# Two matrix products behind an attention stage: tiles that carry the slot from which they can be had, and six more of them at the boundary between the products

## The chip, the cores and the metric

One core of a Trainium2 chip. The metric is device time in microseconds of one execution, the median of several. TensorE multiplies, VectorE (DVE) and ScalarE (ACT) read accumulators, split and add operands, SyncE (SP) issues nearly all DMA transfers, in order, each after what it must wait for.

## What is computed

```python
def _attn_ref(q, k, v):                      # 8 batches, 12 heads, 448 positions, 64 wide
    scores = scale * np.matmul(q, k.transpose(0, 1, 3, 2)) - np.log(S)
    attn = 1.0 / (1.0 + np.exp(-scores))
    return np.matmul(attn, v).astype(np.float32)

def _moe_ref(x, w_in, w_out):                # x [3584, 768], w_in [768, 2048], w_out [2048, 768]
    h = x @ w_in
    g = np.maximum(0.01 * h, h)
    return (g @ w_out).astype(np.float32)
```

The output of the attention, heads side by side, is the `x` of the second function. All in float32; the weights come as float64 and are turned into float32 on the chip.

## The kernel before, in words

There are three stages: attention, the first FFN product (h), the second FFN product. Both FFN products use a bilinear scheme with 20 block products in place of 24: operands are sums and differences of blocks, and accumulators are added into several outputs. Each product runs in four passes `p` over the positions (two batches each), 20 forms `i` per pass, two halves per form: 160 items per product. One item is 12 matmuls 128x128 by 128x448, because each float32 operand is split into a high and a low part (fp32r) and three of the four partial products are made.

The order is written out by hand. Time is counted in slots, one per item; `now` is the slot. `at(when, rank, fn)` (line 169) puts a piece of work into a slot, `slot` (line 176) issues a slot's pieces in order of rank, then the item's matmuls. Every engine then works through its own instructions in that order, and waits where it must.

Operands and results live in tiles of one size, 128x896 float32 (448 KB). `tiles` (line 254) adds tiles to the list `spare`: 13 from the start (`TILES`), 3 more from the first product on (`MORE`), 2 more for the second (`LAST`). `grab` (line 258) takes the first of the list, `drop` (line 265) puts one back at its end. A tile whose last user has not finished may be handed out; the new user then waits.

First product: the weights of forms 15 to 19 are streamed through three buffers in every pass (`Streamed`, tiles `ws`): loaded, high part by a cast on ACT, low part by a subtraction on DVE, in slots given by `prepared_by` (line 698). An accumulator is read into a tile `h` one slot after its item (`read1`); finished blocks are passed through the leaky function on ACT, and stored to memory (`save1`, line 725; `full`); three differences of them, tiles `m`, are made and stored by `made2` (line 770), which drops the tile in the same slot. Beside this, DVE unpacks and sums the weights `w_out` for the second product (`prep`, tiles `wd` and `ws1`), paced by `SHARE` (line 27), into memory; they are loaded again as `w`, in seven groups of four.

Second product: operand `k` (`Operand`, line 798) is loaded (`load`: one or two tiles `g`; a block that the operand before it has is shared), added up into a tile `gf` where it is a sum (`whole`, DVE), cast (`high`, ACT, into a tile `gh` or one of its own) and its low half subtracted (`low`, DVE). Item `k` issues, in this order, the sum of operand k+2, the low half of k+1, the high half of k+2, work on late weights, the reading of a finished accumulator, its own matmuls, and then loads as far as tiles allow: `g_load` (line 887) loads the next operand if the list has tiles for it beside those that `wanted` (line 874) counts, with `SPARE` to spare. The first four operands are placed by the table `FIRST2`: step, operand, how many slots ahead of the boundary, rank. Results are built up in tiles `o`; `store` (line 933) issues the transfer to the output and drops the tile at once. The weights of the last two groups are loaded in the first items of the second product.

## Time and profile before

| what | value |
|---|---|
| runs | 1092.62, 1093.48, 1092.15 us; median 1092.62 |
| the profiled execution | 1088.45 us, its span 1086.7 us |
| TensorE busy | 1039.6 us (96%) |
| DVE, ACT busy | 849.7 us (78%), 575.5 us (53%) |
| DMA | 319.82 MB, mean 294 GB/s |
| chain that ended last | TensorE 68%, DMA 15%, DVE 11% of the span |

The profiled execution is one run, 4.2 us under the median. Attention takes the first 250 us or so, the first FFN product the time to 658 us, the second the rest. A busy TensorE is not TensorE at its peak: matmuls are pipelined, so the count of matmuls in a stretch says more than the busy time. A wait is put down to what came last.

### The profile page before, as it was taken

The page shows a single profiled execution, that of the slowest core. Times are in us where ns is not written, and L with a number is a line of the kernel's source. Part 1 is how long each engine was busy: PE and PEld are TensorE (multiplying, and loading weights), DVE is VectorE, ACT ScalarE, POOL GpSimd, SP SyncE. Part 2 cuts the span into 40 slices and gives each one's busy share as a digit, 9 for nine tenths or more (in the row PEclk, how much of TensorE's full clock was granted, in tenths as well). Part 3 has the DMA queues.
Part 4 walks back from the last instruction along what each step waited for, and adds up shares of the span by engine and source line. Part 5 has one row for each costly group of instructions (what it writes and reads, how often), then busy time and mean ns, then how long its engine had stood idle before and what let it go on. Part 6 is the DMA issues. An engine that isn't in the chain of part 4 may idle for free.

```text
span 1086.7 us, 15679 instructions
## 1 busy us (share of the span) xinstructions
PE 1039.6 (96%) x5690; PEld 859.9 (79%) x5690; DVE 849.7 (78%) x1094; ACT 575.5 (53%) x698; POOL 0.3 (0%) x5
## 2 busy tenths in 40 slices
PE   9999999999999999999999996899899989998998
PEld 5554555547898999899989985799799979988997
DVE  5888889888879787878866785787877877878777
ACT  6877878785644444444447653543344334424442
POOL 0000000000000000000000000000000000000000
PEclk9999999999999999999999997899999999999999
DMA  7899998989949976986798687989958986897796
GB/s 272 281 357 312 319 354 272 400 270 346 332 155 319 338 277 205 337 307 230 238 358 304 220 293 275 332 293 323 355 208 287 355 304 236 292 350 257 252 317 244
DMA packets 123837, 319.82 MB, mean 294 GB/s; under 512 B 12912, under 2 KB 44656, under 8 KB 123760
## 3 DMA queue, kind: packets, MB, share of 16 engines
q1 hardware_dynamic: 123040, 318.13, 83.7%
q8 instruction: 45, 0.74, 0.3%
q10 hardware_dynamic: 720, 0.69, 0.2%
q14 instruction: 32, 0.26, 0.1%
HBM read 221.77 MB, written 96.99 MB: 293 GB/s over the span
## 4 chain that ended last, share of the span: by engine, by line
PE 68%; DMA 15%; DVE 11%; issue 3%; ACT 1%; SPq 1%; DVEq 0%; ACTq 0%
PE f L135 28%; PE pv L135 10%; PE acc_A L135 9%; PE sc L135 9%; DMA g<-g 7%; PE acc_B L135 6%; PE acc_E L135 3%; DMA out<-o 3%; PE acc_D L135 2%; DVE g L135 2%; DVE gf L135 2%; DMA xd<-x_s 1%; PE acc_C L135 1%; SPq L135 1%; DVE wd L135 1%
## 5 line engine op out<-in xcount | busy, mean ns | idle before, releaser
L135 PE MATMUL f<-xh,w 128*128 128x448 f32 x960 | 271.1, 362 | 2.8 <-DVE x L135 1.6
L135 PEld LDWEIGHTS f<-xh,w 128*128 128x128 f32 x960 | 180.0, 188 | 16.6 <-issue 2.2
L135 PE MATMUL f<-xl,w 128*128 128x448 f32 x480 | 173.6, 362 | 0.0
L135 DVE TENSOR_TENSOR gf<-g,g 128x896 f32<-128x896 f32 x104 | 113.3, 1089 | 74.2 <-DMA g<-g 26.4
L135 ACT CAST g<-gf 128x896 fp32r<-128x896 f32 x64 | 60.4, 944 | 143.9 <-DVE gf L135 138.5
L135 ACT ACTIVATE s<-sc 128x896 f32<-128x896 f32 x144 | 119.7, 934 | 9.3 <-PE sc L135 9.0
L135 DVE TENSOR_TENSOR h<-h,f 128x896 f32<-128x896 f32 x88 | 95.5, 1085 | 36.4 <-PE f L135 34.7
L135 PE MATMUL pv<-s,v 128*64 128x448 f32 x576 | 113.8, 543 | 0.0
L135 PE MATMUL acc_A<-g,w 128*128 128x448 f32 x256 | 83.9, 383 | 20.1 <-DVE g L135 19.3
L135 PEld LDWEIGHTS sc<-qks 64*128 64x128 f32 x876 | 79.2, 185 | 28.4 <-issue 16.2
L135 ACT COPY h<-f 128x896 f32<-128x896 f32 x56 | 50.1, 909 | 93.7 <-PE f L135 77.9
L135 PE MATMUL sc<-qks 64*128 64x448 f32 (+1 forms) x876 | 96.6, 368 | 3.2 <-DVE x L135 2.9
L135 PE MATMUL f<-xh,ws 128*128 128x448 f32 x320 | 92.8, 368 | 6.8 <-DVE ws L135 4.5
L135 PE MATMUL acc_A<-gh,w 128*128 128x448 f32 x320 | 95.4, 369 | 0.0
L135 PEld LDWEIGHTS f<-xl,w 128*128 128x128 f32 x480 | 90.0, 187 | 5.8
L135 PE MATMUL acc_B<-gh,w 128*128 128x448 f32 x320 | 93.3, 362 | 0.0
L135 DVE TENSOR_TENSOR xl<-xl,xh 128x896 fp32r<-128x896 f32 x64 | 69.5, 1087 | 26.0 <-ACT xh L135 25.9
L135 PEld LDWEIGHTS pv<-s,v 128*64 128x64 f32 x576 | 39.0, 137 | 63.3 <-issue 51.7
L135 PE MATMUL acc_B<-g,w 128*128 128x448 f32 x256 | 79.2, 365 | 2.6 <-DVE g L135 2.5
L135 ACT ACTIVATE h<-h 128x896 f32<-128x896 f32 x56 | 53.1, 951 | 42.4 <-DVE h L135 41.9
L135 ACT CAST xh<-xl 128x896 fp32r<-128x896 f32 x64 | 60.2, 941 | 26.9 <-PE f L135 19.7
L135 PEld LDWEIGHTS acc_A<-g,w 128*128 128x128 f32 x256 | 49.9, 198 | 27.6 <-DVE g L135 22.9
(76 smaller groups left out, 1597.9 us busy)
## 6 DMA issues: line engine op xcount, KB each, us to landing
g<-g SPq DMA_DIRECT2D x240, 448.0 KB, 5.2
xl<-xd SPq DMA_DIRECT2D x64, 448.0 KB, 5.6
g<-h SPq DMA_DIRECT2D x64, 448.0 KB, 5.7
qk<-in_qk SPq DMA_DIRECT2D x46, 448.0 KB, 6.1
xd<-x_s SPq DMA_DIRECT2D x36, 448.0 KB, 7.3
xd<-x SPq DMA_DIRECT2D x28, 448.0 KB, 7.0
wr<-in_w_in SPq DMA_DIRECT2D x24, 512.0 KB, 5.7
wr<-in_w_out SPq DMA_DIRECT2D x24, 512.0 KB, 4.4
```

The costliest lines, as they stand in the source:

```text
L135: return lambda *args, **kw: tc.keep_in_program_order(issue(*args, **kw))
```

## The change

A place in `spare` is now a tuple: the slot from which the tile can be had, the pool, the tag, and a kind. `grab` takes the place with the smallest of (slot from which it can be had, but not before now; preference by kind). `drop` puts a tile back with `now + slots`: 1 for most, 2 for an `h` whose store was issued a slot before, 3 for tiles whose store is issued in this slot, 4 for stored results of the second product. `room` counts places that can be had by the next slot and are not of the kind RESULTS; `g_load` goes by it.

The two tiles `LAST` are of the kind RESULTS: only `h`, `m` and `o` tiles may take them. They are added 40 slots before the boundary (start of the last pass of the first product) and not at it, with four tiles of the kind LENT, which may be taken until the boundary and are given back at item `BACK` = 10. The room for both is that of the unpacking of `w_out`, which so must be done 40 slots earlier; its pace `SHARE` is raised. The last group of weights takes the room of the four when they are given back, so its loads move from the first items to items 12 to 18; the group before it is loaded at items 1, 3, 5 and 7. `FIRST2` loads the first operands 11 to 6 slots ahead of the boundary instead of 4 to 0, and two more operands by it. The low parts of the streamed weights 18 and 19 come first in their slot (rank -1). The condition `SPARE` is 2.

```diff
--- before.py
+++ after.py
-FAR, SPARE = 8, 3
+FAR, SPARE = 8, 2
+BACK = 10
 FIRST2 = (
-    ("load", 0, 4, 10), ("load", 1, 3, 10), ("whole", 0, 2, 4), ("high", 0, 2, 4), ("load", 2, 2, 10), ("low", 0, 1, 4),
...
+    ("load", 0, 11, 10), ("load", 1, 9, 10), ("load", 2, 7, 10), ("load", 3, 6, 10), ("whole", 0, 6, 4), ("high", 0, 5, 4),
...
-SHARE = 0.88
+SHARE = 0.92
...
-TILES, MORE, LAST = 13, 3, 2
+TILES, MORE, LAST, LOAN = 13, 3, 2, 4
+RESULTS, LENT = 1, 2
...
     spare, homes = [], {}
-    def tiles(stack, name, side, n):
+    def tiles(stack, name, side, n, kind=0):
         pool = stack.enter_context(tc.tile_pool(name=name, bufs=1, side=side, reuse_waits="tile"))
-        spare.extend((pool, f"{name}{i}") for i in range(n))
-    def grab(name, dtype=F32R):
-        pool, tag = spare.pop(0)
+        spare.extend((0, pool, f"{name}{i}", kind) for i in range(n))
+    def grab(name, dtype=F32R, result=False):
+        first = {RESULTS: 0, LENT: 1 + result, 0: 1}
+        place = min((x for x in spare if x[3] != RESULTS or result), key=lambda x: (max(x[0], now), first[x[3]]))
+        spare.remove(place)
+        _, pool, tag, kind = place
         t = pool.tile([P, NB, S], dtype, tag=tag, name=name)
-        homes[id(t)] = pool, tag
+        homes[id(t)] = pool, tag, kind
         return t
-    def drop(t):
-        spare.append(homes.pop(id(t)))
+    def drop(t, slots=1):
+        pool, tag, kind = homes.pop(id(t))
+        spare.append((now + slots, pool, tag, kind))
+    def room():
+        return sum(x[0] <= now + 1 and x[3] != RESULTS for x in spare)
     attn = ExitStack()
     vs = attn.enter_context(tc.tile_pool(name="vs", bufs=4, reuse_waits="tile"))
...
             dma(out=xd[self.p][n], in_=t)
             for x in gone:
-                drop(xs.pop(x))
+                drop(xs.pop(x), 3)
         def start(self):
...
     wb = ctx.enter_context(tc.tile_pool(name="wb", bufs=(len(GROUPS1) - SPLIT1) * KQ, reuse_waits="tile"))
     shift(ctx, "pad3", 64)
     tiles(ctx, "l", "left", MORE)
-    shift(left, "pad4", 192)
+    shift(ctx, "pad4", 192)
     rot = left.enter_context(tc.tile_pool(name="rot", bufs=3, reuse_waits="tile"))
     psum = banks("ps_f", {f"acc{n}": (1, 2) for n in range(4)})
-    def prepared_by(when_, x, load, high=3, low=4):
+    def prepared_by(when_, x, load, high=3, low=4, rank=3):
         at(when_ + load, 6, x.load)
         at(when_ + high, 3, x.high)
-        at(when_ + low, 3, x.low)
+        at(when_ + low, rank, x.low)
     for g in range(SPLIT1, len(GROUPS1)):
         for j in range(KQ):
...
     for p in range(NQ):
         for n in range(15, 20):
             x = ws[p, n] = Streamed(p, n)
-            prepared_by(when(p, 0), x, *((12 + 4 * (n - 15) + y for y in (0, 3, 4)) if n < 18 else (2 * n - 4 + y for y in (0, 2, 3))))
+            prepared_by(when(p, 0), x, *((12 + 4 * (n - 15) + y for y in (0, 3, 4)) if n < 18 else (2 * n - 4 + y for y in (0, 2, 3))), rank=3 if n < 18 else -1)
     use = [(g, u) for g in range(len(TRIPLES)) for u in range(KQ)]
     AHEAD = len(GROUPS1) * KQ
     w2 = {}
...
     def save1(p, jj, x, t, keep=False):
         dma(out=gd[p][x][:, 2 * jj:2 * jj + 2], in_=t)
         if not keep:
-            drop(t)
+            drop(t, 3)
     def read1(p, i, jj):
         chain, _, reads = PRODUCTS1[i]
...
             readings[p, o, jj] = seen
             lone = left1[o] == 1
             if seen == 1:
-                t = outs1[p, o, jj] = grab(f"h_{p}_{o}_{jj}", F32)
+                t = outs1[p, o, jj] = grab(f"h_{p}_{o}_{jj}", F32, True)
                 if lone:
                     leaky(t, acc, sign)
                 else:
...
         for y in got:
             if (p, y, jj) not in over and all(z <= set(got) for z in users if y in z):
                 over.add((p, y, jj))
-                at(now + 3, 9, lambda t=outs1[p, y, jj]: drop(t))
+                at(now + 3, 9, lambda t=outs1[p, y, jj]: drop(t, 2))
     def made2(p, jj, x, a, b):
-        t = grab(f"m_{p}_{x[:2]}_{jj}", F32)
+        t = grab(f"m_{p}_{x[:2]}_{jj}", F32, True)
         (add if "+" in x else sub)(t, outs1[p, a, jj], outs1[p, b, jj])
         at(now + 2, 8, lambda: save1(p, jj, x, t))
...
             n += not x.single and (j == k + 2 or bool(x.first())) and not x.ready
         x = operands[min(k + 2, len(items) - 1)]
         n += x.single or len([m for m in x.new if m not in x.lent]) < 2
-        n += SPARE if k > 6 else 1
+        n += SPARE
         if k and k % 2 == 0:
-            n += sum(y[0] == "c" for y in PRODUCTS[items[k - 1][1]][3])
+            n += max(sum(y[0] == "c" for y in PRODUCTS[items[k - 1][1]][3]) - sum(x[3] == RESULTS for x in spare), 0)
         return n
     def g_load(k, far):
         nonlocal ahead
-        while ahead <= min(far, len(items) - 1) and len(spare) >= len(operands[ahead].new) + wanted(k + 1):
+        while ahead <= min(far, len(items) - 1) and room() >= len(operands[ahead].new) + wanted(k + 1):
             operands[ahead].load()
             ahead += 1
...
     ahead = 1 + max(k for step, k, *_ in FIRST2 if step == "load")
     used = 0.0
+    loan = ExitStack()
     for n, item in enumerate(items1):
+        if n == len(items1) * (NQ - 1) // NQ:
+            assert next(preps, 0) == 0
+            right.close()
+            tiles(ctx, "o", "right", LAST, RESULTS)
+            tiles(loan, "q", "right", LOAN, LENT)
         slot(lambda: first_step(*item))
         for _ in range(2):
             if sums and sums[0][0] <= now:
...
         used = max(used, n * SLOT * SHARE)
         while used < (n + 1) * SLOT * SHARE and next(preps, 0) != 0:
             pass
-    assert next(preps, 0) == 0
     left.close()
-    right.close()
-    tiles(ctx, "o", "left", LAST)
-    shift(ctx, "pad5", 192)
     t2b = ctx.enter_context(tc.tile_pool(name="t2b", bufs=KQ, reuse_waits="tile"))
-    t2c = ctx.enter_context(tc.tile_pool(name="t2c", bufs=KQ, side="right", reuse_waits="tile"))
-    for g, u in use[AHEAD:]:
-        w2[g, u] = Wide(1, g, u, *((t2b, "t2") if len(TRIPLES[g]) == 3 else (t2c, "t1")))
+    for g, u in use[AHEAD:AHEAD + KQ]:
+        w2[g, u] = Wide(1, g, u, t2b, "t2")
+    def end_loan():
+        spare[:] = [x for x in spare if x[3] != LENT]
+        assert all(x[2] != LENT for x in homes.values())
+        loan.close()
+        t2c = ctx.enter_context(tc.tile_pool(name="t2c", bufs=KQ, side="right", reuse_waits="tile"))
+        for g, u in use[AHEAD + KQ:]:
+            w2[g, u] = Wide(1, g, u, t2c, "t1")
+            loads.setdefault(BACK + 2 + 2 * u, []).append(w2[g, u])
     vacant, held = [2, 3, 0, 1], {}
     firsts_at, lasts_at = {}, {}
     for i, (_, chain, _, _) in enumerate(PRODUCTS):
...
     def store(p, o):
         t = outs.pop((p, o))
         dma(out=place(p, o).rearrange("m p s -> p m s"), in_=t)
-        drop(t)
+        drop(t, 4)
     def read(p, i):
         _, chain, _, reads = PRODUCTS[i]
...
         for x in reads:
             how, o = x[0], x[1:3]
             if how == "c":
-                outs[p, o] = grab(f"o{p}_{o}", F32)
+                outs[p, o] = grab(f"o{p}_{o}", F32, True)
                 copy(out=outs[p, o], in_=acc)
             else:
                 t = outs[p, o]
...
             vacant.append(held.pop((p, chain)))
     loads = {}
-    for j in range(len(use) - AHEAD):
-        loads.setdefault(j * 3 // 2, []).append(w2[use[AHEAD + j]])
+    for u in range(KQ):
+        loads.setdefault(1 + 2 * u, []).append(w2[use[AHEAD + u]])
     for k, (p, i, h) in enumerate(items):
         form, chain, _, reads = PRODUCTS[i]
         begins = h == 0 and firsts_at[chain] == i
         ending = k == len(items) - 1
+        if k < BACK:
+            lent = [x for x in spare if x[3] == LENT]
+            spare[:] = [x for x in spare if x[3] != LENT]
+        if k == BACK:
+            end_loan()
         def work():
             early = k + 3 < len(items) and bool(operands[k + 3].first())
             for far, step in ((3, "whole"),) * early + ((2, "whole"), (1, "low"), (2, "high")):
```

**SP's queue at the boundary.** `ws_3_18`, `ws_3_19` are the last streamed weights, `xl15_3` the last operand of the first product, `g_3_n<-h` and `g_3_n<-m` stores of its results; `g11_0_0_0` and `g01_0_0_0` are the two tiles of item 0, with a 1 at the end of item 1, `w1_j_4` late weights. Before:

```order
L135 DMA g_3_4_171<-h_3_10_0_5614 128x896
L135 DMA ws_3_19_6139<-ts_19_65 128x1024
L135 DMA g_3_4_171<-h_3_10_1_5632 128x896
L135 DMA g_3_6_173<-h_3_20_0_5967 128x896
L135 DMA g_3_6_173<-h_3_20_1_5984 128x896
L135 DMA g11_0_0_0_6185<-g_0_5_139 128x896
L135 DMA g01_0_0_0_6187<-g_0_1_135 128x896
L135 DMA g_3_2_169<-h_3_30_0_5652 128x896
L135 DMA g_3_9_176<-m_3_20_0_6161 128x896
L135 DMA g11_0_0_1_6208<-g_0_5_139 128x896
L135 DMA g01_0_0_1_6210<-g_0_1_135 128x896
```

With the change:

```order
L138 DMA g11_0_0_0_6049<-g_0_5_139 128x896
L138 DMA g01_0_0_0_6051<-g_0_1_135 128x896
L138 DMA w1_0_4_6068<-t1_0_66 128x2x384
L138 DMA xl14_3_6070<-xd_3_14_132 128x896
L138 DMA g_3_0_167<-h_3_00_1_5796 128x896
L138 DMA w1_1_4_6089<-t1_1_67 128x2x384
L138 DMA g11_0_0_1_6091<-g_0_5_139 128x896
L138 DMA g01_0_0_1_6093<-g_0_1_135 128x896
L138 DMA ws_3_18_6110<-ts_18_62 128x1024
L138 DMA w1_2_4_6112<-t1_2_68 128x2x384
L138 DMA xl15_3_6114<-xd_3_15_133 128x896
```

The loads of items 0 and 1 stood behind the last streamed weights and among the stores of the last results; they now stand ahead of `ws_3_18`.

**DVE at the last streamed weights.** `h_3_30_0<-...f10_3_14` reads an accumulator of item -6, `ws` rows are low halves of weights, `gf_0_0_n` is the sum for item n, `g01_0_0_0<-gf` the low half of item 0. Before:

```order
L135 TENSOR_TENSOR h_3_30_0_5652<-h_3_30_0_5652,f10_3_14_6025 128x896
L135 TENSOR_TENSOR ws_3_18_6095<-ws_3_18_6095 128x1024
L135 TENSOR_TENSOR w1_1_4_6078<-w1_1_4_6078 128x768
L135 TENSOR_TENSOR m_3_20_0_6161<-h_3_20_0_5967,h_3_10_0_5614 128x896
L135 TENSOR_TENSOR h_3_30_1_5671<-h_3_30_1_5671,f11_3_14_6042 128x896
L135 TENSOR_TENSOR xl15_3_6099<-xl15_3_6099,xh15_3_6155 128x896
L135 TENSOR_TENSOR w1_2_4_6097<-w1_2_4_6097 128x768
L135 TENSOR_TENSOR m_3_20_1_6182<-h_3_20_1_5984,h_3_10_1_5632 128x896
L135 TENSOR_TENSOR h_3_21_0_5926<-h_3_21_0_5926,f10_3_18_6189 128x896
L135 TENSOR_TENSOR ws_3_19_6139<-ws_3_19_6139 128x1024
```

With the change:

```order
L138 TENSOR_TENSOR gf_0_0_0_6155<-g11_0_0_0_6049,g01_0_0_0_6051 128x896
L138 TENSOR_TENSOR ws_3_18_6110<-ws_3_18_6110 128x1024
L138 TENSOR_TENSOR h_3_30_0_5659<-h_3_30_0_5659,f10_3_14_6032 128x896
L138 TENSOR_TENSOR w1_1_4_6089<-w1_1_4_6089 128x768
L138 TENSOR_TENSOR m_3_20_0_6183<-h_3_20_0_5974,h_3_10_0_5621 128x896
L138 TENSOR_TENSOR h_3_30_1_5678<-h_3_30_1_5678,f11_3_14_6053 128x896
L138 TENSOR_TENSOR xl15_3_6114<-xl15_3_6114,xh15_3_6177 128x896
L138 TENSOR_TENSOR w1_2_4_6112<-w1_2_4_6112 128x768
L138 TENSOR_TENSOR g01_0_0_0_6051<-gf_0_0_0_6155,g11_0_0_0_6049 128x896
L138 TENSOR_TENSOR gf_0_0_1_6204<-g11_0_0_1_6091,g01_0_0_1_6093 128x896
L138 TENSOR_TENSOR m_3_20_1_6207<-h_3_20_1_5991,h_3_10_1_5639 128x896
L138 TENSOR_TENSOR ws_3_19_6158<-ws_3_19_6158 128x1024
```

`ws_3_19` moved ahead of the reading of `h_3_21_0`, `ws_3_18` ahead of that of `h_3_30_0`; two sums and a low half of the second product came in between.

**SP's queue at the end of a period of 40 items.** `g11_0_19_n`, `g10_0_19_n` are the tiles of items 38 and 39, `out_0<-o0_20` the store of a result, `g11_1_0_0` and `g01_1_0_0` the tiles of item 40. Before:

```order
L135 DMA g11_0_19_0_7016<-g_0_5_139 128x896
L135 DMA g10_0_19_0_7018<-g_0_4_138 128x896
L135 DMA out_0<-o0_20_6769 128x2x448
L135 DMA g11_0_19_1_7037<-g_0_5_139 128x896
L135 DMA g10_0_19_1_7039<-g_0_4_138 128x896
L135 DMA g11_1_0_0_7041<-g_1_5_150 128x896
L135 DMA g01_1_0_0_7043<-g_1_1_146 128x896
```

With the change:

```order
L138 DMA g11_0_19_0_6998<-g_0_5_139 128x896
L138 DMA g10_0_19_0_7000<-g_0_4_138 128x896
L138 DMA g11_0_19_1_7019<-g_0_5_139 128x896
L138 DMA g10_0_19_1_7021<-g_0_4_138 128x896
L138 DMA out_0<-o0_20_6772 128x2x448
L138 DMA g11_1_0_0_7040<-g_1_5_150 128x896
L138 DMA g01_1_0_0_7042<-g_1_1_146 128x896
```

The two loads of item 39 now stand ahead of the store.

## Rows read from the trace of the kernel before

**Rows 1.** Page, part 1: busy us (share of the span) xinstructions by engine.
```profile
PE 1039.6 (96%) x5690; PEld 859.9 (79%) x5690; DVE 849.7 (78%) x1094; ACT 575.5 (53%) x698; POOL 0.3 (0%) x5
```

**Rows 2.** Chain that ended last, 618 to 790 us: start us, us, what.
```profile
718.23 4.88 PE acc_B L135 x23
723.11 4.80 PE acc_A L135 x24
```

**Rows 3.** By stage: from:to, us, PE, PEld, DVE, ACT, POOL busy (x), PEclk, DMA share, GB/s.
```profile
250.00:640.00 390.00, 382.96 (x1911) 353.50 (x1908) 305.78 (x405) 197.44 (x227) 0.00 (x0) 1.00 0.82 286
605.00:620.00 15.00, 15.00 (x77) 14.06 (x76) 9.51 (x10) 10.67 (x13) 0.00 (x0) 1.00 0.40 137
620.00:625.00 5.00, 5.00 (x27) 4.69 (x26) 3.82 (x5) 2.62 (x3) 0.00 (x0) 1.00 0.99 273
640.00:720.00 80.00, 63.99 (x267) 55.80 (x266) 56.34 (x58) 33.66 (x41) 0.00 (x0) 0.85 0.82 290
660.00:670.00 10.00, 5.12 (x13) 4.07 (x14) 4.91 (x6) 2.68 (x3) 0.00 (x0) 0.51 0.99 333
720.00:760.00 40.00, 40.00 (x201) 37.22 (x200) 31.22 (x31) 16.75 (x19) 0.00 (x0) 1.00 0.94 329
745.00:755.00 10.00, 10.00 (x52) 9.37 (x51) 8.15 (x9) 3.60 (x5) 0.00 (x0) 1.00 0.99 373
760.00:800.00 40.00, 35.20 (x171) 31.32 (x170) 31.12 (x31) 17.20 (x19) 0.00 (x0) 1.00 0.82 296
850.00:900.00 50.00, 45.15 (x216) 41.12 (x215) 38.75 (x38) 19.23 (x21) 0.00 (x0) 0.97 0.86 312
950.00:1000.00 50.00, 44.83 (x213) 40.68 (x212) 39.09 (x39) 18.09 (x20) 0.00 (x0) 0.97 0.90 327
```

**Rows 4.** TensorE in order of time: start us, us, what [idle before <-releaser].
```profile
350.88 0.68 PE L135 MATMUL f<-xh,ws 128*128 128x448 f32 x2 [0.85 <-DVE ws L135]
...
641.48 0.47 PE L135 MATMUL f<-xh,ws 128*128 128x448 f32 x1 [0.59 <-DVE h L135]
646.49 1.11 PE L135 MATMUL f<-xh,ws 128*128 128x448 f32 x2 [1.93 <-DVE ws L135]
658.38 0.47 PE L135 MATMUL acc_E<-g,w 128*128 128x448 f32 x1 [3.22 <-ACT g L135]
661.36 4.47 PE L135 MATMUL acc_E<-g,w 128*128 128x448 f32 x11 [2.52 <-DVE g L135]
669.72 0.74 PE L135 MATMUL acc_A<-g,w 128*128 128x448 f32 x1 [3.52 <-DVE g L135]
686.27 0.47 PE L135 MATMUL acc_A<-g,w 128*128 128x448 f32 x1 [2.37 <-DVE g L135]
...
774.43 2.47 PE L135 MATMUL acc_A<-g,w 128*128 128x448 f32 x11 [3.38 <-DVE g L135]
```

**Rows 5.** Waits from 600 to 720 (SP), 640 to 1087 (DVE): us in total, times, longest.
```profile
SPq L135 <- DMA g<-m: 26.7, 5, 6.7
...
DVE gf L135 <- DMA out<-o: 22.2, 10, 4.5
```

**Rows 6.** SP's queue in order of time, 600 to 720 us: start us, us, what.
```profile
642.81 7.06 SPq L135 DMA_DIRECT2D g<-g  x2
```

**Rows 7.** Chain that ended last, 618 to 790 us, a store of a result.
```profile
766.34 5.82 DMA out<-o
```

**Rows 8.** DVE in order of time, columns as in rows 4.
```profile
636.35 1.08 DVE L135 TENSOR_TENSOR h<-h,f 128x896 f32<-128x896 f32 x1
...
645.22 1.22 DVE L135 TENSOR_TENSOR ws<-ws 128x1024 fp32r<-128x1024 f32 x1
...
772.28 1.09 DVE L135 TENSOR_TENSOR gf<-g,g 128x896 f32<-128x896 f32 x1 [3.96 <-DMA out<-o]
```

**Rows 9.** DMA issues, 600 to 720 us: xcount, KB each, median us to landing.
```profile
g<-g SPq DMA_DIRECT2D x32, 448.0 KB, 6.3
```

**Rows 10.** Waits of DVE from 250 to 660 us, columns as in rows 5.
```profile
DVE wd L135 <- DMA t<-wd: 11.9, 4, 4.4
```

More of the change, by code (lines that the diff above doesn't have):

```diff
@@ L18 @@
 P = 128
-FAR, SPARE = 8, 3
+FAR, SPARE = 8, 2
+BACK = 10
 FIRST2 = (
-    ("load", 0, 4, 10), ("load", 1, 3, 10), ("whole", 0, 2, 4), ("high", 0, 2, 4), ("load", 2, 2, 10), ("low", 0, 1, 4),
-    ("whole", 1, 1, 4), ("high", 1, 1, 4), ("load", 3, 0, 10))
+    ("load", 0, 11, 10), ("load", 1, 9, 10), ("load", 2, 7, 10), ("load", 3, 6, 10), ("whole", 0, 6, 4), ("high", 0, 5, 4),
+    ("low", 0, 4, 4), ("whole", 1, 4, 4), ("high", 1, 3, 4), ("low", 1, 2, 4), ("load", 4, 2, 10), ("whole", 2, 3, 4),
+    ("high", 2, 2, 4), ("whole", 3, 2, 4), ("high", 3, 1, 4), ("load", 5, 1, 10))
 ROOM = 1.3, 2.1, 2.1, 1.0, 0.7
-SHARE = 0.88
+SHARE = 0.92
 SLOT = 2.42
```

## The prediction

> **What bounds it now.** First the page: TensorE is busy 96% of the span [rows 1], but that counts a matmul in the pipeline as busy; what it could do is read from the rate. Two operand items of the second FFN product (24 matmuls) take 4.80 us where nothing holds them [rows 2], so one item, 12 matmuls, is 2.4 us, and I number the 160 items of the second product from 0, those of the first from -160 to -1. The table by stage [rows 3] then gives what is lost: in 250 to 640 us 1911 matmuls at 0.2 us fill 382 of 390 us; from 720 to 760 nothing is missing; but 760 to 800, 850 to 900 and 950 to 1000 hold 171, 216 and 213 matmuls and so lose 5.8, 6.8 and 7.4 us, 20.0 in sum. At the boundary item -3 starts at 641.48 [rows 4] and item 18 at 718.23 [rows 2]: 76.8 us for 21 items worth 50.4, so **26.4 us are lost at the boundary**. Together 46 us. The rest of the program is not touched by a wait that this change could take away, but for the weights below.
>
> Why the boundary loses it: TensorE waits six times, 14.2 us in all, mostly for the low halves of operands and weights on DVE [rows 4], and in between it runs slow: from 660 to 670, right after the waits of 3.22 and 2.52 us, the granted clock is 0.51 of full speed, nearly all of it the lower of its two levels, 1.2 and 2.4 GHz [rows 3, 4]. Behind them stands SP's queue: five times it stood until a store g<-m had landed, 26.7 us in all [rows 5]; two loads g<-g took it 7.06 us to pass [rows 6]. The pool code says why. The first free tile is handed out, and a tile is free at the moment its store is *issued*. Followed by hand, g01_0_0_1, the low half of item 1, gets the tile of m_3_20_0 in the same slot in which that is stored, three more loads of the first items do the same, and a fourth does it a slot later.
>
> Why the periods of 40 items lose it: the same rule. gf_1_0_0, the sum for item 40, gets the tile of o0_11 one slot after its store is issued. The store takes 5.82 us [rows 7], the sum on DVE starts at 772.28 after 3.96 us of waiting [rows 8], the low half of item 39 stands behind it in DVE's queue, and TensorE goes on with item 39 at 774.43 after 3.38 us [rows 4]. DVE's waits for out stores: 22.2 us, ten times [rows 5].
>
> **The change, term by term.**
>
> *Boundary.* Removed: the tiles of stored results may be had 2 to 4 slots later, and six more tiles (four of them until item 10) are there, so no load of items 0 to 13 now takes a tile whose store was issued in that slot or the one before. The loads of items 0 to 3 stand before the last streamed weights in SP's order; items 0 and 1 find DMA time: from 605 to 620 the engines are at 0.40 [rows 3]. What is late next:
> (1) ws_3_19, the weights of items -2 and -1. It now leads its slot, but DVE has the low half of item 0 and the sum of item 1 ahead of it. From h_3_30_0, which starts at 636.35 in the trace [rows 8], nine operations stand before it, seven at 1.00 and two at 0.87 us start to start; that puts it at 645.1 against 645.22 now [rows 8]. So this wait stays: about 2.9 us against the pace without one.
> (2) Items 0 to 5 are loaded early; DVE's chain of sums ends the low half of item 3 some 0.4 us late.
> (3) DMA. A 448 KB transfer at full share costs 1.23 us (373 GB/s, 745 to 755) to 1.38 us (333 GB/s, 660 to 670) [rows 3]; I take 1.3, the middle. Item -12 starts near 619.3 (641.48 less the wait of 0.59 and nine items). From there to the tile of item 4, 25 transfers stand in SP's new order, 32.4 us with the smaller weights counted by size: done near 652. Behind it stand 12 more up to item 7's tile, 15.2 us: near 667, item 6's 1.3 before, and cast and low half add 2 us. Item 6, due at 665.8, is 2 us late; in the same way items 8 and 9, two tiles each, lose 1.4 and 0.6, and items 19 and 20, behind an out store and two pieces of weights, 1.5.
>
> Sum of the waits: 2.9+0.4+2+1.4+0.6+1.5 = 8.8 us. Before, six waits of 14.2 us went with 26.4 us lost, so the slow clock and refilling added 0.86 us to each us waited. From 760 to 800, with one long wait of 3.38 us, the clock stays at 1.00 [rows 3, 4]. Mine are short but several; I take half, 0.4: 12.3 us stay. **Gain 14.1 us**; bounds 9 (the full 0.86) and 20 (1.23 us per transfer, no slow clock).
>
> The Trainium skill (DMA: Bandwidth & Descriptors, "Measured (HBM→SBUF, 128 partitions, SWDGE, issued from GpSimd)") has 425 GB/s for 16 MB on one core; by it a transfer would be 1.08 us and, as an estimate from that page, the sum some 5 us better. The rows with full share do not reach it over 10 us, so their 1.3 is used.
>
> *Periods.* gf_1_0_0 and its like (items 18, 31, 38, 40 of each period) now get tiles that were not just stored; two tiles are kept for results alone, so a result does not drive operands out. Items 35 to 39 are loaded a slot sooner, and those of item 39 no longer behind the store of o0_20, which waits for DVE. What is late next is DMA again: items 30 to 41 need 24 loads with two stores among them, 26 x 1.3 = 33.8 us in a stretch of 28.8; tiles let SP run some 3 items ahead, which covers all but about 1.5 us. The second tile of item 33 now waits for item 28 where it waited for 27: 0.7 us more. I leave 2.3 us per period, 6.9 in three. **Gain 13.1 us**; bounds 6 (loads that land as late as at the boundary, 6.3 us after issue [rows 9], instead of 5) and 18.
>
> *Streamed weights.* In passes 0 to 2 the low half of ws_19 comes ahead of one sum, worth 1.0 us on DVE; the wait is 0.85 us in each of them (the first [rows 4]; two more like it). **Gain 2.6 us**; bounds +3 and -3, since more DVE work now lies in these passes.
>
> *At nothing:* the raised pace (the unpacking of w_out must be done by item -40): about 3 us of DVE work moves ahead of it, in a stage where DVE has 306 of 390 us [rows 3]. Uncovered it costs those 3 us. The later loads of the last two groups of w_out: 8 loads, used from item 30 on; they only thin the crowd at items 9 and 10. The tail after the last item is as before.
>
> Sum: 14.1+13.1+2.6 = 29.8, say **30 us**. The profiled execution took 1088.45 us, which would become 1058.5. It lies 4.2 us under the median of the runs, 1092.62; the forecast goes from the median: **1062.5 us**.
>
> **Rivals.**
> *DMA takes the place of the tiles.* For it: the share is 0.94 to 0.99 in just these stretches [rows 3]. At 1.5 us per transfer (from 620 to 625 the engines move 273 GB/s at 0.99, 1.68 us for 448 KB [rows 3], with weights in short packets among them; 1.5 is halfway to 1.38) 26 transfers take 39 us in 28.8, and the periods gain nothing; the boundary gains 9, weights 2: 1081. Against: 745 to 755 moves 373 GB/s. Chance 0.15.
> *All waits but the first go*, clock full: boundary 22, periods 17, weights 3: 1051. Chance 0.10.
> *Too few tiles: slower.* Two of 18 tiles can hold results only. If a two-tile item's load were then let go by item k-4 instead of k-5 or k-6, landing (6.3 us at the boundary [rows 9]), sum, cast and low half (3.3 us) and the item itself would make four items last 12.0 us, not 9.6. Over the 24 crowded items of each of four periods that is 58 us; less the 17 of boundary and weights and the 20 that the periods lose today: 1114. It decides as soon as loads in the crowded stretches wait for item k-4. Against: in the new order they are let go by k-5 and k-6. Chance 0.04.
> *It does not do what it says*: tiles come from other stores just as late, or DVE's four waits for the unpacked weights' stores (11.9 us, [rows 10]) fall on TensorE where one in four does now; 0 to 9 us either way of no change: 1092. Chance 0.06.
>
> **How the numbers follow.** The forecast has 0.65; its own range is 1055 to 1072, from the bounds of its terms that do not all fall together. The range over the cases, **1052 to 1079**, leaves out the slower and idle cases, most of the DMA case and half of the best: about 0.2. A measurement here tells 0.2%, 2.2 us, from no change. Faster: 0.65+0.15+0.10+0.01 = 0.91; within it 0.04; slower 0.05.
>
> **What would show it.** SP's waits on g<-m and DVE's on out<-o nearly gone; item 18 near 703 where it is at 718, less what earlier stages gain; a granted clock over 0.85 through the boundary; in the three windows, moved with the shift, some 2 us lost each. TensorE's first wait (ws) at the boundary still there. Wrong if gf still waits for out<-o, if DVE's waits for g<-g grow past the 26 us of today, or if TensorE waits anew between items 8 and 30, where the loaned tiles are gone.

## The result, and the profile after

The change takes 1054.18 us (median of 1053.19, 1055.18, 1057.70 and 1052.08), the kernel before 1093.05 beside it: a ratio of 0.964, 95% interval 0.961 to 0.968. Measured again (c0 below) it is 0.967 (0.965 to 0.969). Predicted were 1062.5 us in a range of 1052 to 1079. The forecast's own range, 1055 to 1072, is just missed on the fast side. The profiled execution took 1053.19 us, 35.3 less than that of the kernel before; the medians lie 38.9 apart, since the profiled execution of before was 4.6 us under its median and this one 1.0.

From the page of the change, part 1 (columns as in [rows 1]), where TensorE was at 96%:

```profile
PE 1029.6 (98%) x5690; PEld 854.1 (81%) x5690; DVE 847.9 (81%) x1094; ACT 576.2 (55%) x698; POOL 0.3 (0%) x5
```

TensorE of the change in order of time, the waits over 0.4 us that are left from 460 us to item 18, and three rows without a wait: at 640.99, 641.30 and 701.16 (columns as in [rows 4]):

```profile
466.40 0.47 PE L138 MATMUL f<-xl,w 128*128 128x448 f32 x1 [2.25 <-DVE xl L138]
...
638.21 0.44 PE L138 MATMUL f<-xh,ws 128*128 128x448 f32 x1 [1.48 <-ACT h L138]
...
640.99 0.47 PE L138 MATMUL f<-xh,ws 128*128 128x448 f32 x1
641.30 0.36 PE L138 MATMUL f<-xl,ws 128*128 128x448 f32 x1
...
647.00 0.67 PE L138 MATMUL f<-xh,ws 128*128 128x448 f32 x2 [2.93 <-DVE ws L138]
...
658.83 0.48 PE L138 MATMUL acc_A<-g,w 128*128 128x448 f32 x1 [0.47 <-DVE g L138]
661.96 0.48 PE L138 MATMUL acc_A<-g,w 128*128 128x448 f32 x1 [0.45 <-DVE g L138]
670.37 0.47 PE L138 MATMUL acc_A<-gh,w 128*128 128x448 f32 x1 [1.13 <-ACT o L138]
674.51 0.47 PE L138 MATMUL acc_A<-g,w 128*128 128x448 f32 x1 [1.27 <-DVE g L138]
...
701.16 0.36 PE L138 MATMUL acc_B<-gh,w 128*128 128x448 f32 x1
```

First find where the items start. The wait of 1.48 us now stands ahead of item -4, not -3: its first matmul is that of the row at 638.21, and 12 matmuls further item -3 starts, at **640.99** (before 641.48). Item 18 starts with the row at 701.16 (the prediction had it near 703). For the kernel before, the prediction took the chain's row at 718.23 for its start [rows 2], but that row has 23 matmuls: the first of the 24 comes ahead of a wait of 0.65 us. Item 18 of before starts at **717.22**, and three waits over 0.4 us, the last of them inside item 18, stand beside the six of the prediction. TensorE of the kernel before:

```profile
690.63 0.74 PE L135 MATMUL acc_E<-g,w 128*128 128x448 f32 x1 [0.55 <-DVE g L135]
...
698.10 0.47 PE L135 MATMUL acc_C<-g,w 128*128 128x448 f32 x1 [0.68 <-DVE g L135]
...
717.22 0.37 PE L135 MATMUL acc_B<-gh,w 128*128 128x448 f32 x1
718.23 0.47 PE L135 MATMUL acc_B<-g,w 128*128 128x448 f32 x1 [0.65 <-DVE g L135]
```

Item -3 to item 18 took 75.7 us before, takes 60.2 now, and is worth 50.4 at the rate without waits: **25.3 us were lost at the boundary, 9.8 are now**, 15.6 gained. From item 18 to the end of the span it was 369.4 us and is 350.2: **19.2 gained**. Ahead of item -3 only 0.5 are gained. 15.6 + 19.2 + 0.5 is the whole difference.

The table by stage for the change (columns as in [rows 3]): a stretch ahead of the boundary, the boundary, and the periods, moved with the shift:

```profile
460.00:470.00 10.00, 7.75 (x32) 6.78 (x31) 5.02 (x8) 1.03 (x2) 0.00 (x0) 0.85 0.78 300
630.00:640.00 10.00, 8.52 (x43) 7.67 (x42) 8.66 (x10) 7.13 (x9) 0.00 (x0) 1.00 1.03 408
640.00:650.00 10.00, 6.94 (x29) 5.76 (x28) 10.00 (x11) 4.98 (x6) 0.00 (x0) 0.90 0.72 274
650.00:660.00 10.00, 9.54 (x44) 8.44 (x44) 7.31 (x8) 4.46 (x5) 0.00 (x0) 0.93 0.96 328
660.00:670.00 10.00, 8.79 (x43) 7.56 (x41) 5.06 (x6) 3.10 (x4) 0.00 (x0) 1.00 0.99 358
670.00:680.00 10.00, 8.30 (x39) 7.11 (x40) 8.24 (x9) 5.85 (x8) 0.00 (x0) 1.00 1.03 404
680.00:690.00 10.00, 10.00 (x52) 9.37 (x51) 9.98 (x11) 6.84 (x9) 0.00 (x0) 1.00 1.01 385
745.00:785.00 40.00, 39.68 (x197) 36.41 (x196) 32.40 (x33) 18.29 (x20) 0.00 (x0) 1.00 0.86 335
835.00:885.00 50.00, 49.88 (x247) 45.74 (x246) 42.36 (x42) 23.01 (x26) 0.00 (x0) 1.00 0.89 335
935.00:985.00 50.00, 48.92 (x241) 44.60 (x240) 40.28 (x40) 22.12 (x25) 0.00 (x0) 1.00 0.87 320
```

The three stretches at the periods' ends hold 197, 247 and 241 matmuls where 200, 250 and 250 fit; before they held 171, 216 and 213 [rows 3]. The granted clock at the boundary is 0.90 of full speed at the lowest (0.51 in [rows 3]), most of it the higher of the two levels.

Waits: SP for stores of `m` from 600 to 720 us, and DVE's sums from 640 us on (columns as in [rows 5]):

```profile
SPq L138 <- DMA g<-m: 0.6, 1, 0.6
```

```profile
DVE gf L138 <- DMA g<-g: 16.7, 23, 1.7
```

The 26.7 us of SP and the 22.2 us of DVE for stores of results [rows 5] are gone; the latter have no row any more.

### The profile page after: what moved, and what is told of

Same layout as the page of the kernel before. It is cut to its first block, busy times and chain, and to the rows that moved or that the text cites. A ratio compares the mean times of both kernels' runs of the same rounds, so it can differ in the third digit from the quotient of the medians.

```text
span 1051.4 us, 15669 instructions
## 1 busy us (share of the span) xinstructions
PE 1029.6 (98%) x5690; PEld 854.1 (81%) x5690; DVE 847.9 (81%) x1094; ACT 576.2 (55%) x698; POOL 0.3 (0%) x5
## 4 chain that ended last, share of the span: by engine, by line
PE 79%; DMA 9%; DVE 8%; issue 2%; ACT 1%; SPq 1%; ACTq 0%; DVEq 0%
PE f L138 30%; PE pv L138 10%; PE sc L138 10%; PE acc_B L138 9%; PE acc_A L138 9%; DMA g<-g 5%; PE acc_D L138 4%; PE acc_C L138 3%; PE acc_E L138 3%; DVE gf L138 1%; DMA xd<-x_s 1%; DVE g L138 1%; DMA t<-wd 1%; SPq L138 1%; DVE wd L138 1%
## 5 line engine op out<-in xcount | busy, mean ns | idle before, releaser
L138 PE MATMUL acc_A<-gh,w 128*128 128x448 f32 x320 | 93.2, 362 | 1.1 <-ACT o L138 1.1
L138 PE MATMUL acc_A<-g,w 128*128 128x448 f32 x256 | 79.6, 366 | 3.2 <-DVE g L138 2.3
L138 ACT CAST xh<-xl 128x896 fp32r<-128x896 f32 x64 | 60.2, 940 | 23.3 <-PE f L138 11.6
L138 PEld LDWEIGHTS f<-xh,ws 128*128 128x128 f32 x320 | 60.8, 190 | 11.5 <-DVE ws L138 3.3
```

What stands on the lines that cost most here:

```text
L138: return lambda *args, **kw: tc.keep_in_program_order(issue(*args, **kw))
```

## The experiments

Each was run beside the kernel before on one chip; ratios are to that. The kernel before took 1087.9 to 1093.1 us in these groups, so ratios can be compared from row to row, and medians only within a group (c0, e15, e13 and e17 are one). Three numbers of each profiled execution tell where its time lies: the start of item -3, what is lost from there to the start of item 18 (the time less 50.4 us), and item 18 to the end of the span. Each comes from one execution. How far two executions can differ ahead of item -3 the table shows as well: c0, e8, e15 and e2 have the change's program up to there and reach it between 640.6 and 646.7 us.

| kernel | median us, ratio (95%) | item -3 at | lost to item 18 | item 18 to end |
|---|---|---|---|---|
| before | 1093.05 | 641.5 | 25.3 | 369.4 |
| the change | 1054.18, 0.964 (0.961-0.968) | 641.0 | 9.8 | 350.2 |
| c0: the change again | 1053.38, 0.967 (0.965-0.969) | 640.6 | 9.5 | 351.3 |
| e1: before + choice by slot | 1074.12, 0.988 (0.983-0.992) | 642.9 | 19.3 | 358.9 |
| e20: before + SPARE 2 | 1085.02, 0.996 (0.994-0.999) | 642.5 | 25.9 | 363.7 |
| e13: before + both | 1067.16, 0.980 (0.977-0.983) | 640.7 | 18.0 | 350.5 |
| e15: change, SPARE 3 | 1067.04, 0.978 (0.976-0.980) | 642.1 | 9.7 | 364.4 |
| e2: change, out stores at once | 1067.61, 0.980 (0.976-0.985) | 646.7 | 8.8 | 361.9 |
| e8: change, room in any slot | 1055.38, 0.970 (0.967-0.974) | 641.8 | 10.8 | 351.1 |
| e5: change, first loads later | 1056.96, 0.972 (0.968-0.975) | 643.9 | 12.2 | 350.0 |
| e3: change, old rank of ws | 1057.74, 0.972 (0.969-0.975) | 643.5 | 10.5 | 350.0 |
| e17: change, ws a slot sooner | 1058.16, 0.971 (0.969-0.973) | 644.8 | 8.7 | 350.2 |
| e24: change, late weights later | 1051.90, 0.966 (0.963-0.970) | 642.7 | 7.0 | 350.2 |
| e25: e24 + ws, last pass only | 1052.31, 0.967 (0.964-0.969) | 641.4 | 6.1 | 351.5 |

Several expectations count "item -3" from the row at 638.21, which is item -4, and item 18 of before from 718.23. Where they say that the change takes 63 us to item 18, gained 13.7 us there or has 12.7 us left, read 60.2, 15.6 and 9.8; for its gain of 18.4 us from item 18 on read 19.2, and for the 9.8 of e1 10.6. The theory is that of the prediction: young stores in handed-out tiles. The main rival is that tiles kept for results, or more of them, do it.

### e1: the choice alone

In the kernel before, `spare` holds (slot, pool, tag); all else as it was.

```diff
-        pool, tag = spare.pop(0)
+        place = min(spare, key=lambda x: max(x[0], now))
+        spare.remove(place)
+        _, pool, tag = place
...
-    def drop(t):
-        spare.append(homes.pop(id(t)))
+    def drop(t, slots=1):
+        spare.append((now + slots, *homes.pop(id(t))))
```

(`drop(..., 3)`, `2` and `4` at the four places as in the change.)

> The kernel before, with one part of the change: a dropped tile carries the slot from which it can be had, and a new user takes the one that can be had first; the room test still counts all free tiles, and there are no more tiles, no tiles for results alone and no earlier loads. Theory (it is the young store in the tile that costs): the sum for item 40 of each period no longer sits in a tile stored a slot before, so the periods gain nearly all of the 18.4 us that item 18 to the end gained with the change, 14 to 18 us; at the boundary the loads of the first items still come late and four tiles less are there, so most of the 13.7 us gained there stay lost, 0 to 5 us back. In sum 1070 to 1078 us, and DVE's waits of a sum for a stored result, 22.2 us in the kernel before, under 3. Rival (the tiles kept for results and the test of room by slot do it): the periods gain under 6 us and the time is 1085 or more.

1074.12 us: the time is as the theory has it, its parts are not. DVE's sums wait for no store `out<-o` any more (two waits for `g<-m`, 6.1 us, are left at the boundary), but the periods gain 10.6 us, not 14 to 18, and the boundary 6.0. The gain is uneven: in the first period a wait of 2.88 us is left at 765.14, in the two that follow none is over 1.3. The rival's 6 us are passed as well: something else gives the other half. Tiles' owners, followed by hand through the pool code, gave the next idea: the crowded items 73 to 79 are still let go 3 items ahead, 75 to 79 of them 4 ahead with the change.

### e15, e13, e20: the number SPARE

e15 is the change with `SPARE` 3 for 2, e13 is e1 with `SPARE` 2, e20 the kernel before with `SPARE` 2:

```diff
-FAR, SPARE = 8, 2
+FAR, SPARE = 8, 3
```

(e15; e13 and e20 the other way.)

> The change with one number put back: SPARE 3 in place of 2, the tiles that must stay over when the next operand is loaded. Followed by hand through the pool code, items 73 to 79 (and their like in each period) are then let go 3 items ahead, as in the kernel before, where the change lets items 75 to 79 go 4 ahead; items 58 to 63 as well go a slot later. The first study of the parts showed that the choice by slot alone gives 9.8 of the 18.4 us that the change gains from item 18 on. Theory (the rest of that gain is the one slot of lead in the crowded stretches, and SPARE gives it): this kernel loses 6 to 9 us against the change, all of it after item 18, as waits of TensorE for low halves behind sums that wait for loads. Rival (the rest comes from the tiles kept for results): within 2 us of the change.

> The kernel before with the choice by slot and SPARE 2, without tiles for results alone, without the test of room by slot, without earlier loads or more tiles. Its loads run 4 items ahead in the crowded stretches, as with the change. Theory: from item 18 to the end it takes what the change takes, 350 us, within 2; the boundary stays at about 70 us from item -3 to item 18 (63 with the change), the streamed weights are as before: 8 to 13 us above the change in sum. Rival (tiles for results alone are what the rest needs): it stays where the choice alone was, 16 to 21 us above the change.

> The kernel before with one number changed, SPARE 2 in place of 3: loads run 4 items ahead in the crowded stretches, but tiles are still handed out first come, first served. The sum for item 39 or so, and for item 9 of a period, then sit in a tile stored a slot before, and loads of items 40 to 45 as well. Theory (choice by slot and lead of the loads each count by themselves, and the wait for a stored result stays): about half of the periods' 18 us is gained, 6 to 11 us, boundary and weights as before: 0.990 to 0.995 of the kernel before; DVE's waits of a sum for a stored result stay above 10 us. Rival (lead is all that the periods lacked): 0.982 to 0.986, the whole 16 to 19 us.

e15 loses 13.7 us against c0 on the same chip, more than expected, and its table by stage (columns as above) puts them in the periods:

```profile
740.00:780.00 40.00, 37.64 (x177) 33.97 (x176) 32.83 (x33) 16.84 (x19) 0.00 (x0) 0.96 0.88 322
830.00:880.00 50.00, 46.32 (x225) 41.36 (x225) 39.41 (x38) 19.32 (x21) 0.00 (x0) 1.00 0.90 330
930.00:980.00 50.00, 46.99 (x224) 42.58 (x223) 40.11 (x40) 19.33 (x21) 0.00 (x0) 0.97 0.92 336
```

SP's waits after 720 us suggest how, first of the change, then of e15, then of e13:

```profile
SPq L138 <- PE acc_A L138: 60.7, 28, 5.0
...
SPq L138 <- DVE g L138: 10.9, 9, 3.2
```

```profile
SPq L138 <- DVE g L138: 53.9, 38, 4.2
SPq L138 <- PE acc_A L138: 45.6, 24, 4.3
```

```profile
SPq L135 <- DVE g L135: 25.5, 23, 2.0
```

My reading, which no run parts from others: let go an item later, the loads take the sum tile that a low half on DVE has yet to read, and SP stands behind that low half (65.4 us of this in the kernel before); let go an item sooner, they take tiles that the matmuls of a finished item have left, and SP waits for TensorE, which is the pace anyway. This wait alone does not price the loss: e13 has 25.5 us of it, the change 10.9, and both take the same time from item 18 on. In e13, without tiles for results, without the test of room by slot and without more tiles, that is 350.5 us, the change's 350.2: in this execution choice and lead are all that the periods needed. One caution: it (1061.4) is the fastest of e13's six runs, whose median is 13.8 us above c0 where I expected 8 to 13; what the slower runs lose, and where, no trace shows.

e20 gains 4.1 us by the medians, 5.7 from item 18 on in its trace, a little under the 6 to 11 that I had put; its sums still wait for stored results, as expected:

```profile
DVE gf L135 <- DMA out<-o: 16.6, 6, 3.6
```

So in the periods the lead alone gives 5.7 us, the choice alone 10.6, both 18.9 (one execution each): together a little more than the sum of the two.

### e2: tiles of stored results at once

```diff
-        drop(t, 4)
+        drop(t, 0)
```

> The change, but the tile of a result of the second product may be had again in the slot in which its store is issued (0 in place of 4); all else stays. Here three loads per period, not sums, get such tiles: the second tile of item 40, one of item 42 and one of item 45, 0 or 1 slots after the store. Theory: the wait moves to the queue of loads, about 5 us each, of which the lead of some three items covers most for one load, but not for three in ten items: 1 to 4 us per period, three periods, 1057 to 1066 us; the boundary is as in the change, within 1 us. Rival (the reserved tiles do it, the age of a store nothing): within 2 us of the change, 1052 to 1056.

1067.61 us, a little over the range; item 18 to the end takes 11.7 us more. SP's waits after 720 us have the row that the change has not:

```profile
SPq L138 <- DMA out<-o: 44.1, 9, 8.9
```

There are nine waits of about 5 us, three per period as expected, and 3.9 us are lost per period. The change's time and these 11.7 us would lie in the range; the profiled execution (1069.61) besides reached item -3 5.7 us later than the change's, with the same program up to there. A load that stands in SP's queue holds all that follow: these nine held it 44.1 us. Followed by hand, the loads of items 73 to 79 also go 3 ahead here, so this run does not part the wait from the lead; it shows that tiles kept for results do not replace the age.

### e8: room in any slot

```diff
-        return sum(x[0] <= now + 1 and x[3] != RESULTS for x in spare)
+        return sum(x[3] != RESULTS for x in spare)
```

> The change, but the test of room counts every free tile that is not kept for results, whether or not it can be had by the next slot; the choice among tiles still goes by slot. Loads are let go a slot or two sooner, and some into tiles stored one slot before, at the boundary only (six such against four); in the periods no tile with a store younger than three slots is taken. Theory: within 2 us of the change, 1052 to 1057, with at most 2 us lost at the boundary and nothing in the periods. Rival (it is the loads held back by the test of room that keep the queue of loads free): 1060 or more, lost in the periods.

1055.38 us, 0.970 (0.967 to 0.974): in the traces 1.0 us more is lost at the boundary, 0.9 in the periods. By them the test of room by slot is worth some 2 us; the ratios, taken on different chips, can't say more.

### e5: first loads later

```diff
-    ("load", 0, 11, 10), ("load", 1, 9, 10), ("load", 2, 7, 10), ("load", 3, 6, 10), ("whole", 0, 6, 4), ("high", 0, 5, 4),
-    ("low", 0, 4, 4), ("whole", 1, 4, 4), ("high", 1, 3, 4), ("low", 1, 2, 4), ("load", 4, 2, 10), ("whole", 2, 3, 4),
+    ("load", 0, 7, 10), ("load", 1, 6, 10), ("load", 2, 4, 10), ("load", 3, 3, 10), ("whole", 0, 3, 4), ("high", 0, 3, 4),
+    ("low", 0, 2, 4), ("whole", 1, 2, 4), ("high", 1, 2, 4), ("low", 1, 1, 4), ("load", 4, 2, 10), ("whole", 2, 3, 4),
```

> The change, but the first four operands are loaded 7, 6, 4 and 3 slots ahead of the boundary (11, 9, 7 and 6 in the change; 4 to 0 before), and their sums, high and low halves follow as late as they can; the six more tiles stay. Theory: DMA at full share is the bound from the last streamed weights to item 9 or so, so the idle DMA time before them is lost: four items with two tiles each are loaded some 4 slots later, about 8 transfers by 1.1 to 1.3 us, 9 to 10 us, of which the lead takes up about half: 3 to 7 us slower than the change, 1057 to 1061 us, lost ahead of item 18. Rival (tiles without a young store are enough, and the early loads only fill the queue earlier): within 1.5 us of the change; or even faster, since fewer sums then stand ahead of the last weights on DVE: the wait of 2.93 us for them would fall under 1.

1056.96 us, just under the range; 2.5 us more are lost at the boundary than in the change. Both ideas show in the trace: the wait for the last weights falls to 0.90 us, and one of 4.59 comes for item 3 at 663.32. By the trace the early loads are worth some 2.5 us.

### e3, e17: the streamed weights

e3 undoes the rank; e17 puts the low halves a slot sooner.

```diff
-... (2 * n - 4 + y for y in (0, 2, 3))), rank=3 if n < 18 else -1)
+... (2 * n - 4 + y for y in (0, 2, 3))), rank=3)
...
-... (2 * n - 4 + y for y in (0, 2, 3))), rank=3 if n < 18 else -1)
+... (2 * n - 4 + y for y in (0, 2, 2))), rank=3 if n < 18 else 3.5)
```

> The change, but the low halves of the streamed weights 18 and 19 have their old place in their slot (rank 3, behind the reading of an accumulator). Theory, as in the prediction: the wait of 0.85 us for the weights returns in each of passes 0 to 2, 2.6 us in sum, and at the boundary the reading of item -6 or so comes ahead of the first weights (the wait of 1.48 us falls to 0.6) while the last weights come a microsecond later (2.93 grows to 3.9): 2 to 3.5 us slower than the change. Rival (the order within a slot only moves waits about): within 1 us of the change.

> The change, but the low halves of streamed weights 18 and 19 are put a slot sooner, into the slot of their high halves, ahead of that slot's work on the second product's operands (rank 3.5; in the change at the head of the slot behind). In the trace of the change the high half of the last one is there at 639.8 us and DVE starts the low half at 645.73, TensorE waits 2.93 us for it; now it would stand four operations, some 4 us, further ahead. The one before moves ahead of the sum of item 0, which stood in front of it and of the reading of an accumulator for which TensorE waits 1.48 us. Theory (an order on DVE is all that wait is): both waits go but for some 0.5 us, the low halves of items 0 and 1 come a microsecond later and have that time; 1.5 to 4 us faster than the change. Rival: the wait moves to the sums of items 0 to 3 behind it: within 1 us of the change, or up to 2 slower if passes 0 to 2 wait for the high half on ACT.

e3's TensorE in order of time has exactly the waits expected:

```profile
349.65 0.68 PE L138 MATMUL f<-xh,ws 128*128 128x448 f32 x2 [0.85 <-DVE ws L138]
...
650.47 1.12 PE L138 MATMUL f<-xh,ws 128*128 128x448 f32 x2 [3.93 <-DVE ws L138]
```

The wait of 0.85 us stands in the other two passes as well, and that of 1.48 falls to 0.58. The kernel reaches item 18 3.2 us after the change and 3.9 after c0; that alone is within what executions differ by, and the rows are the firmer sign. Its ratio is 0.005 above c0's, on another chip.

e17 is 4.8 us slower than c0, where I expected it faster; the rival gives only part of it. The 2.93 us at the weights go, 2.44 come at item 2 (0.46 in c0): 8.7 us lost where c0 loses 9.5, as the rival has it. But it reaches item -3 4.2 us later than c0, and for part of that its trace has a cause. There is no wait for high halves on ACT to speak of (0.2 us); DVE stands for the store of unpacked `w_out`, as in this row of e17's DVE, and `xl` behind it keeps TensorE for 2.28 us, which no other run has there:

```profile
368.89 0.43 DVE L138 TENSOR_SCALAR wd<-wr 128x512 int32<-128x512 int32 x1 [8.70 <-DMA t<-wd]
369.24 1.08 DVE L138 TENSOR_TENSOR xl<-xl,xh 128x896 fp32r<-128x896 f32 x1
```

### e24, e25: a version that beats both?

e24 loads the last two groups of weights later, and puts the first loads ahead of their slot's stores (rank 2 for all six); e25 adds e17's edit for the last pass alone.

```diff
-            loads.setdefault(BACK + 2 + 2 * u, []).append(w2[g, u])
+            loads.setdefault(BACK + 9 + 2 * u, []).append(w2[g, u])
...
-        loads.setdefault(1 + 2 * u, []).append(w2[use[AHEAD + u]])
+        loads.setdefault(BACK + 1 + 2 * u, []).append(w2[use[AHEAD + u]])
...
-    ("load", 0, 11, 10), ...
+    ("load", 0, 11, 2), ...
```

> The change with two more edits at the boundary. The weights of the last two groups of the second product, which are used from item 30 on, are loaded at items 11 to 17 and 19 to 25 (in the change the first group at items 1 to 7, the second at 12 to 18), so four transfers, some 4 us at 1.1 us per 448 KB, leave the crowd of items 1 to 9. And the first six operands' loads stand ahead of their slot's stores in the queue of loads (rank 2, not 10): in the trace of the change that queue stands 6.83 us at 634.91 for results that are not there yet, and DMA falls to a share of 0.72 from 640 to 650. Theory (what stays at the boundary, 12.7 us, is partly loads that come late): the waits of 1.13 and 1.27 us at 670 and 674 go, with the slow refilling behind them 2 to 4 us are gained, and nothing is lost at items 9 to 30. Rival (the loads only move the crowd): within 1.5 us of the change, with new waits of TensorE between items 10 and 30.

> The change with the weights of the last two groups loaded at items 11 to 25 and the first loads ahead of their slot's stores (as in the run before, where the waits at 670 and 674 us went and item -3 to item 18 took 60.3 us, 63 with the change), and besides, in the last pass of the first product alone, the low halves of streamed weights 18 and 19 a slot sooner (in all passes this cost waits for the high half in passes 1 and 2, and at the boundary took away 2.93 us and gave 2.4 us to sums that came late behind loads). Theory: with the loads thinned out the sums of items 0 to 3 have no late load behind them, so the 2.93 us go for good: item -3 to item 18 in 57 to 59 us, in sum 1 to 3 us better than the run before: a ratio to the kernel before of 0.962 to 0.965. Rival (DVE is full there, so what the weights gain the first items lose): 60 us or more, 0.966 to 0.968, as the change.

In e24's trace the waits of 1.13 and 1.27 us at 670 and 674 are gone (0.31 is the most there), nothing over 0.4 comes up to item 30, and the loss at the boundary falls from 9.8 to 7.0 us; in e25's to 6.1 (59.5 us counted as in the expectation, between its two cases). There the 2.93 us for the weights turn into 2.45 at item 2 and 1.09 come back at 671.58; DVE is busy 9.82 of the 10 us from 650 (7.49 in e24), so for that edit the rival holds. In the time neither can be told from the change: 0.966 and 0.967 against c0's 0.967. What executions differ by ahead of item -3 hides it. I take neither as better.

## Why the prediction was right, and which steps were off

The gain came from where it was said, and larger: by the profiled executions 35.3 us for 29.8. The periods' term came out above its upper bound (19.2 for 13.1, at most 18), so there the mechanism was right and the size was not; the time lies below the forecast's own range and inside the stated one because that took in half of the better case.

**Boundary: 15.6 us for 14.1.** *(1)* the wait for `ws_3_19`: 2.9 us forecast, 2.93 measured. *(2)* item 3: 0.4 forecast, 0.45. *(3)*, the loads, is the mis-sized term: items 6, 8, 9, 19 and 20 were to be 5.5 us late; measured are 1.13 ahead of item 6 (ACT's reading of its accumulator), 1.27 in item 7 and nothing over 0.4 at 8, 9, 19 or 20. Item 2's 0.47 was not forecast. In sum the waits are 6.25 us for 8.8. Beyond them 3.5 us go, 0.57 per us waited, where I took 0.4: the two errors work against each other, which was luck. e24, with waits of 3.85 us, loses 7.0, so this factor is no constant. The 0.86 that I had for before comes of the row at 718.23: with the waits at 690.63 and 698.10, and without the 0.59 that stands ahead of item -3, it is 14.8 us of waits and 25.3 lost, 0.71 per us waited. The lower bound, 9, is by the prediction's own numbers 10.

The price of a transfer was too high in most stretches. At full share the change's engines move 408, 404 and 385 GB/s in three stretches of the boundary, so 448 KB take 1.12, 1.14 and 1.19 us, not 1.3; in the fourth, from 660 to 670, they move 358, which is 1.28. In the first period (columns as in [rows 3]) they move 382 to 410, 1.12 to 1.20 us:

```profile
730.00:740.00 10.00, 10.00 (x52) 9.38 (x51) 7.82 (x8) 3.49 (x4) 0.00 (x0) 1.00 1.03 382
740.00:750.00 10.00, 10.00 (x51) 9.17 (x50) 9.46 (x11) 3.78 (x4) 0.00 (x0) 1.00 1.01 397
750.00:760.00 10.00, 9.68 (x48) 8.49 (x47) 9.76 (x10) 4.65 (x5) 0.00 (x0) 1.00 1.03 410
760.00:770.00 10.00, 10.00 (x52) 9.37 (x51) 7.14 (x8) 5.09 (x6) 0.00 (x0) 1.00 1.00 392
```

The kernel before had such a stretch too; I had read two of its rows and taken the middle. Its DMA from 720 us to the end in 40 slices of 9.2 us (busy share in tenths, then GB/s) has 408 in the seventh, at a share of 0.9 or more:

```profile
DMA  9899799966677989999981947979989994676797
GB/s 340 264 331 380 290 350 408 330 220 225 247 240 261 309 264 369 351 344 386 322 332 57 336 157 249 371 234 345 354 337 342 390 347 164 197 270 198 266 353 222
```

The Trainium skill's 425 GB/s (DMA: Bandwidth & Descriptors, "Measured (HBM→SBUF, 128 partitions, SWDGE, issued from GpSimd)"), by which a transfer is, as an estimate, 1.08 us, was nearer than my rows, but no 10 us of the rows above reach it. For these transfers, issued by SP, the measured 1.12 to 1.28 decide.

Which part does it: the choice alone takes 6.0 of the 15.6 us (e1), 1.3 more come with SPARE 2 (e13), e5 gives 2.5 to the early loads, each by one execution, and the rest, some 6, goes with the six tiles, the later weights and the order at the last streamed weights. I did not part these, so for that rest the cause is not shown.

**Periods: 19.2 us for 13.1.** That DVE's sum for item 40 waits for a store, and that this costs TensorE, was right: e1 takes those waits away and gains 10.6. The failed step is "What is late next is DMA again", 33.8 us of transfers in 28.8. At 1.12 to 1.20 us the 26 transfers are 29.1 to 31.2, the share of DMA in the three stretches is 0.86 to 0.89 where I feared it full, and the three lose 3.0 us where I left 6.9. The second failing is one of attribution: I counted the slot of lead for items 35 to 39 as a fact of the new order and never asked which edit gives it. It is SPARE, and putting that back alone costs 13.7 us (e15). The tiles kept for results, which I named as the cause, were not needed in e13's execution. With SPARE 3 they may even cost: item 18 to the end takes 364.4 us in e15 and 358.9 in e1, which has neither them nor the test of room by slot; no run parts these two.

**Streamed weights and stages ahead: 0.5 us for 2.6.** Executions of one program differ by up to 6 us here, so the 0.5 says little; the waits say more. The term itself was right: the three waits of 0.85 us are gone, and come back in e3. What failed is the step "At nothing: the raised pace". DVE's waits for stores of unpacked weights, 11.9 us, longest 4.4 [rows 10], are now 15.5, longest 8.7, and that one falls on TensorE. DVE of the change:

```profile
464.91 0.43 DVE L138 TENSOR_SCALAR wd<-wr 128x512 int32<-128x512 int32 x1 [8.68 <-DMA t<-wd]
465.26 1.08 DVE L138 TENSOR_TENSOR xl<-xl,xh 128x896 fp32r<-128x896 f32 x1
```

TensorE waits 2.25 us for that `xl` at 466.40, and the 10 us from 460 hold 32 matmuls, not 50: 3.6 us lost. A shorter wait of the kind, at 434.96 in the kernel before, is gone; there the 20 us from 420 held 92 matmuls, now 101. The longest such wait is 3.9 to 4.4 us in all four kernels at the old pace and 8.4 to 10.2 in all ten at the new; up to the last pass of the first product e13 and e3 issue the same work but for the pace (some buffers lie elsewhere in memory), and have 4.0 and 8.9. I priced the pace by DVE's work, and not by the stores that the work must wait for; that the waits may fall on TensorE I had put into a rival. Besides, the low half of `ws_3_18`, now ahead of the reading of an accumulator, makes item -4 wait 1.48 us, where item -3 waited 0.59; with the old rank it is 0.58 again (e3).

**Rivals.** DMA did not take the place of the tiles. "All waits but the first go" came closer in the time than the forecast (1051 and 1062.5 for 1054.18); it holds for the periods, not for the boundary or the stages ahead. Too few tiles: not with SPARE 2; in e15, where loads go one item later, 13.7 us are lost.

## What to carry to other kernels

A pool that hands out tiles in the order of their return treats a tile whose store was just issued like a free one: let tiles carry the time from which they are free, and choose by it. Ask of each held-back load which rule held it and whose reader then frees its tile: without the item of lead, the rest of this change kept only 22 of its 36 us (e15 and c0). Work that is sped up in idle time is priced by its waits too, not by its busy time alone.

## What the runs showed of the hardware that I had not expected

At the same share of 0.99 to 1.03, one core's DMA moves anything from 333 [rows 3] to 410 GB/s over 10 us, so the share alone does not price a transfer. And the granted clock does not follow from the length of one wait: with that of 2.25 us at 466 it is 0.85 from 460 to 470 in the profiled execution of the change; in that of c0, with as much of those 10 us idle, it stays at 1.00, and in the 10 us behind them too:

```profile
460.00:470.00 10.00, 7.65 (x39) 6.83 (x38) 4.19 (x7) 2.01 (x3) 0.00 (x0) 1.00 0.89 332
```
